# An S4 backward pass woven into an FFN: small gradient stores as rows, parameter work moved out of the middle phase, turns and sums a step apart

## Chip, cores and metric

One core of a Trainium2 chip. The metric is the device time of one execution in microseconds (us), median of several runs. TensorE, VectorE, ScalarE, GpSimd and SyncE appear in the profile as PE (matmuls) and PEld (weight loads), DVE, ACT, POOL and SP. All runs quoted here are in the same (fast) state; the granted TensorE clock of each is named where it matters.

## The reference

The function is a sum of two branches over a layer norm of `u` (2048 x 576): an S4 convolution and a gated FFN of width 4608. The kernel returns the output and twelve gradients (cut):

```python
def _A_ref(u, A_re, A_im, B_re, B_im, C_re, C_im, log_dt, Dskip):   # the six: (576, 128); the last two: (576,)
    dt = jnp.exp(log_dt)[:, None]
    logdA = dt * (A_re + 1j * A_im)
    dB = dt * (B_re + 1j * B_im)
    P = jnp.exp(logdA[:, :, None] * l[None, None, :])               # l = 0..2047
    K = jnp.einsum("dn,dnl,dn->dl", C_re + 1j * C_im, P, dB).real
    ...                                                              # y = irfft(rfft(u) * rfft(K)), padded to 4096
    return y + u * Dskip[None, None, :]
...
return x + _A_ref(xn, ...) + _B_ref(xn, W_gate, W_up, W_down)        # xn = layernorm(x)
# wanted: the value and jax.vjp of it with grad_out
```

## The kernel before

The FFN's matmuls are the backbone. The S4 branch is a Python generator whose steps are emitted between them: each `yield` gives the step's estimated us, and a pace loop asks for the next step while S4's sum lags behind `PACE` times the FFN's. Phase 1 takes FFTs of the inputs, phase 2 builds the kernel K and the sums for the parameters' gradients, in five chunks of 128 channels, phase 3 does the rest of the convolution. Both branches share every engine's in-order queue. In the cuts, dk is the gradient with respect to K; a turn is the transposing of Y into YT, and the sums are the matmuls at L760 that read YT and dkc.

```python
while s4_open and stt < PACE * (ft - start):          # PACE = 0.93
    r = next(sgen, None)
    ...
        stt += r

# the end of phase 1
for n2 in range(ST):                                  # 16 steps
    o = up.tile([P, D], BF16, name="dk_o")
    for hs, ps in self.back2(bp, "dk", n2):           # loads bC from C_dk (2 buffers), multiplies
        g.bal.copy(o[:, hs], ps, DH)
    nc.sync.dma_start(self.dk_dram[:, n2, :], o[:])
    yield 0.5

# phase 2
for k, d0, dsz in dchunks():                          # 5 chunks
    raw = rawp.tile([P, 6, N], BF16, name="raw")
    for i, nm in enumerate(names):
        nc.sync.dma_start(raw[:dsz, i, :], self.aps[nm][d0:d0 + dsz, :])
    ...                                               # ldt, dt = exp, VectorE products -> pw
    Tt = par2.tile([P, 4, P], F32, name="Tt")
    ps = self.ps()
    for i in range(4):
        nc.tensor.transpose(out=ps[:, i * P:i * P + dsz], in_=pw[:dsz, i, :], ...)   # L666
    ...
    for s0 in range(0, dsz, SC):                      # 32 channels
        dkc = parp.tile([P, 2, ST, SC], BF16, name="dkc")
        nc.sync.dma_start(dkc[:, 0, :, :], self.dk_dram[:, :, dd0:dd0 + SC])
        nc.gpsimd.tensor_tensor(dkc[:, 1, :, :], dkc[:, 0, :, :], lv..., op=ALU.mult)
        ...                                           # ex, X, XC; for each 4 channels E, Y
                if len(pend) > 1:
                    self.group(pend.pop(0), ytp, gp)
                    yield 1.5
    ...
    yield from self.param_grads(d0, dsz, raw, dt, Tt, Sm, parp, par2, gp)

def group(self, item, ytp, gp):
    ...                                               # matmuls for K, copy to Kst
    ...                                               # 8 transposes of Y into PSUM
    YT = ytp.tile([P, 2, DG, P], BF16, name="YT")
    bal.copy(YT[:]..., tb, 2 * DG * P, fp32=False)
    ...
    nc.tensor.matmul(gv[:, dl, :, ri, :], lhsT=YT[:, ri, dl, :], rhs=dkc[:, :, :, dd + dl], ...)  # L760
    ...                                               # VectorE: pr = X * sums; Sm = reduce(pr)

# the end of param_grads
dldb = pool.tile([P, 1], BF16, name="dldb")
v.tensor_scalar(dldb[:dsz], tot[:dsz], dtk, None, op0=ALU.mult)
nc.sync.dma_start(self.outs["log_dt"][d0:d0 + dsz].rearrange("(p o) -> p o", o=1), dldb[:dsz])
```

The skip gradient is stored the same way, once near the start, by five stores of one bf16 element per partition from GpSimd's queue.

## Time and profile before

| | before |
|---|---|
| time, median of 6 runs | 2232.35 us (2230.11 to 2234.6) |
| profiled span, mean clock | 2232.9 us, 0.946 |
| TensorE / VectorE / ScalarE busy | 86 / 66 / 68% |

TensorE is the busiest engine, so the reader looks for where it idles. The prediction below shows the page, TensorE's waits, the windows at the dips and the slow transfers.

### The profile page before, as it was taken

Reading aid. Unit: us, or ns where it says so; the run is one execution under the profiler, and the core shown is the slowest. Engines: PE = TensorE matmul, PEld = TensorE weight load, DVE = VectorE, ACT = ScalarE, POOL = GpSimd, SP = SyncE. Lnnn points to the kernel's source line nnn. Section 1 sums busy time; section 2 is a strip of 40 time slices with the busy share of each in tenths; the row PEclk is TensorE's granted clock in tenths of the full one; section 3 lists DMA queues with packets and bytes.
Section 4 is the critical chain, followed back from the end, with each engine's and each line's share of the span. In section 5 each row is a group of like instructions: output and inputs, shape, how many; then the busy total and the mean of one; then the engine's idle time right before and its main releaser. Section 6 shows DMA issues by size and latency. Waiting matters only on the chain. (4 is left out here: it accounts for less than half of the span.)

```text
span 2232.9 us, 45610 instructions
## 1 busy us (share of the span) xinstructions
PE 1929.9 (86%) x17720; PEld 1316.7 (59%) x17720; DVE 1471.0 (66%) x3464; ACT 1518.7 (68%) x3293; POOL 233.0 (10%) x300
## 2 busy tenths in 40 slices
PE   6989999848996999878999699996988998789877
PEld 3665667435754666645666476664665566457545
DVE  7434664499866988569786698747943775652464
ACT  4755766479966979759978699946955764353462
POOL 5210000001100101101101000200100010010010
PEclk9989999969997999989999899998999999899999
DMA  9587889604645644734645554635468996896697
GB/s 281 179 215 243 242 239 274 172 8 94 145 100 78 127 114 95 149 75 74 130 113 97 90 117 106 132 99 78 88 142 262 259 257 209 273 317 140 159 248 203
DMA packets 244169, 358.67 MB, mean 161 GB/s; under 512 B 88880, under 2 KB 153520, under 8 KB 243184
## 3 DMA queue, kind: packets, MB, share of 16 engines
q1 hardware_dynamic: 213136, 292.04, 43.8%
q0 software_dynamic: 28704, 61.36, 18.9%
q8 instruction: 138, 2.26, 0.4%
q10 hardware_dynamic: 2112, 2.36, 0.3%
q14 instruction: 79, 0.65, 0.1%
HBM read 211.21 MB, written 144.48 MB: 159 GB/s over the span
## 5 line engine op out<-in xcount | busy, mean ns | idle before, releaser
L65 ACT CAST osx<-ps_mm 128x288 bf16<-128x288 f32 x711 | 270.6, 430 | 88.3 <-PE ps_mm L278 78.7
L283 POOL DMA_DIRECT2D acc_dram<-osx x176 | 152.2, 865 | 1387.8 <-ACT osx L65 1098.7
L278 PE MATMUL ps_mm<-wgT,dgT 128*128 128x288 bf16 x1152 | 218.8, 291 | 9.0 <-DVE upm L243 5.4
L278 PE MATMUL ps_mm<-wuT,duT 128*128 128x288 bf16 x1152 | 217.4, 291 | 0.0
L312 PEld LDWEIGHTS <-xs 128*128 128x128 bf16 x1536 | 151.1, 100 | 109.5 <-issue 15.8
L278 PE MATMUL ps_mm<-wd,hT 128*128 128x288 bf16 x1152 | 190.8, 291 | 22.8 <-ACT upb L241 16.3
L234 PE MATMUL ps_mm<-xT,wg 128*128 128x512 bf16 x720 | 204.2, 389 | 6.7 <-ACT osx L65 3.9
L234 PE MATMUL ps_mm<-xT,wu 128*128 128x512 bf16 x720 | 200.4, 387 | 1.4 <-ACT osx L65 1.1
L234 PE MATMUL ps_mm<-gT,wdT 128*128 128x512 bf16 x720 | 194.3, 387 | 8.1 <-DVE upm L243 8.1
L298 PE MATMUL ps_mm<-gq,hN 128*128 128x144 bf16 x2304 | 169.1, 231 | 22.0 <-DMA gq<-gq_dram 15.0
L764 DVE TENSOR_TENSOR pr<-X,ps_s 128x256 f32<-128x256 f32 x288 | 108.7, 418 | 107.2 <-PE ps_s L760 105.4
L298 PEld LDWEIGHTS <-hN 128*128 128x128 bf16 x2304 | 157.3, 100 | 31.2 <-issue 16.4
L243 DVE SCALAR_TENSOR_TENSOR upm<-ps_mm,upb 128x512 bf16<-128x512 f32 x144 | 99.0, 687 | 91.0 <-ACT upb L241 90.7
L312 PE MATMUL ps_mm<-dgN,xs 128*128 128x384 bf16 x768 | 151.7, 339 | 5.7 <-DMA xs<-xs_dram 5.7
L65 ACT COPY YT<-ps_s 128x1024 bf16<-128x1024 bf16 x140 | 146.4, 1046 | 9.0 <-PE ps_s L753 7.8
L65 ACT CAST obw<-ps_mm 128x384 bf16<-128x384 f32 x101 | 48.2, 478 | 149.8 <-PE ps_mm L312 112.2
L278 PEld LDWEIGHTS <-hT 128*128 128x128 bf16 x1152 | 110.6, 99 | 60.9 <-issue 23.7
L312 PE MATMUL ps_mm<-duN,xs 128*128 128x384 bf16 x768 | 141.5, 330 | 0.0
L278 PEld LDWEIGHTS <-dgT 128*128 128x128 bf16 x1152 | 113.1, 100 | 40.9 <-issue 11.8
L278 PEld LDWEIGHTS <-duT 128*128 128x128 bf16 x1152 | 113.5, 100 | 29.3
L760 PE MATMUL ps_s<-dkc,YT 128*128 128x32 bf16 x1152 | 88.7, 232 | 45.3 <-POOL dkc L677 19.7
L760 PEld LDWEIGHTS <-YT 128*128 128x128 bf16 x1152 | 66.2, 111 | 90.0 <-ACT YT L65 65.2
(245 smaller groups left out, 4262.0 us busy)
## 6 DMA issues: line engine op xcount, KB each, us to landing
acc_dram<-osx POOLq DMA_DIRECT2D x192, 288.0 KB, 5.6
gT<-gT_dram SPq DMA_DIRECT2D x44, 640.0 KB, 6.2
xT<-xT_dram SPq DMA_DIRECT2D x44, 640.0 KB, 5.4
gq<-gq_dram SPq DMA_DIRECT2D x48, 576.0 KB, 4.2
xs<-xs_dram SPq DMA_DIRECT2D x48, 512.0 KB, 3.8
out_dram<-obw SPq DMA_DIRECT2D x96, 96.0 KB, 2.7
base_dram<-base SPq DMA_DIRECT2D x16, 576.0 KB, 4.6
f_base<-base_dram SPq DMA_DIRECT2D x16, 576.0 KB, 5.8
```

The costliest lines, as they stand in the source:

```text
L65: self.nc.scalar.copy(out, in_)
L234: nc.tensor.matmul(ps[:], lhsT=w[:, k, fs], rhs=rhs[:, k, :], start=(k == 0), stop=(k == NK - 1))
L243: nc.vector.scalar_tensor_tensor(upm[:], ps_g[:], 0.0, upb[:], op0=ALU.is_gt, op1=ALU.mult)
L278: nc.tensor.matmul(ps[:, :DH], lhsT=lt[:, js], rhs=rh, start=(i == 0), stop=(i == len(mms) - 1))
L283: nc.gpsimd.dma_start(g.acc_dram[:, t, :, :], o[:], accum_op=ALU.add)
L298: nc.tensor.matmul(ps[:, (ft - f) * 144:(ft - f + 1) * 144], lhsT=self.hN[:, st, ft * P:(ft + 1) * P], rhs=gq[:, st, :], start=(st == 0), ...
L312: nc.tensor.matmul(ps[:, :Fc], lhsT=xs[:, st, :], rhs=src[:, st, :], start=(st == 0), stop=(st == ST - 1))
L760: nc.tensor.matmul(gv[:, dl, :, ri, :], lhsT=YT[:, ri, dl, :], rhs=dkc[:, :, :, dd + dl], start=True, stop=True)
L764: nc.vector.tensor_tensor(pr[:], X[:, dx:dx + DG, r0:r0 + 2].rearrange("p d r a -> p d (r a)").unsqueeze(2).to_broadcast(sh), psg[:, 0:DG ...
```

## The change

The intent: store the small gradients as rows through a transpose; take the raw parameters out of phase 2, with the transposed values and the summed gradients going through memory (`T_dram`, `R_dram`); put one step between turning Y and the sums that read it; let the GpSimd copy dk into the operand instead of the load writing it. The core of the diff:

```diff
-PACE = 0.93
+PACE = 0.95
+def store_rows(g, pool, cols, out):
+    ps = g.psum_s4.tile([P, 512], F32, name="ps_s4")
+    nc.tensor.transpose(out=ps[:NK, 0:P], in_=cols, identity=g.ident_f[:])
+    rowb = pool.tile([NK, P], BF16, name="rowb")
+    nc.vector.tensor_copy(rowb[:], ps[:NK, 0:P])
+    nc.sync.dma_start(out[0:full * P].rearrange("(k p) -> k p", p=P), rowb[0:full, :])
+    nc.sync.dma_start(out[full * P:D].rearrange("(k p) -> k p", k=1), rowb[full:NK, 0:D - full * P])
 def dskip_out(g, small):
-    for k, d0, dsz in dchunks():
-        nc.gpsimd.dma_start(g.out_dskip[d0:d0 + dsz].rearrange("(p o) -> p o", o=1), totb[:dsz, k:k + 1])
+    store_rows(g, small, tot[:], g.out_dskip)
 ... (phase 1)
+        yield from self.params()        # raw loads, products, transposes; Tt stored to T_dram
 ... (phase 2, per chunk)
-                raw, ldt, dt, pw, transposes, copy to Tt
+                nc.sync.dma_start(Tt[:, :, 0:dsz], self.T_dram[:, :, d0:d0 + dsz])
+                    dkr = parp.tile([P, ST, SC], BF16, name="dkr")
+                    nc.sync.dma_start(dkr[:], self.dk_dram[:, :, dd0:dd0 + SC])
-                    nc.sync.dma_start(dkc[:, 0, :, :], self.dk_dram[:, :, dd0:dd0 + SC])
+                    nc.gpsimd.tensor_copy(dkc[:, 0, :, :], dkr[:])
+                            if len(turned) > 0:
+                                self.sums(turned.pop(0), gp)
+                                yield 0.8
                             if len(pend) > 1:
-                                self.group(pend.pop(0), ytp, gp)
-                                yield 1.5
+                                turned.append(self.turn(pend.pop(0), ytp))
+                                yield 0.7
-                yield from self.param_grads(d0, dsz, raw, dt, Tt, Sm, parp, par2, gp)
+                nc.sync.dma_start(self.R_dram[:, :, d0:d0 + dsz], R[:, :, :dsz])
 ... (end of param_grads)
-        nc.sync.dma_start(self.outs["log_dt"][d0:d0 + dsz].rearrange("(p o) -> p o", o=1), dldb[:dsz])
+        v.tensor_scalar(g.dld[:dsz, k:k + 1], tot[:dsz], dtk, None, op0=ALU.mult)
+        if k == NK - 1:
+            store_rows(g, pool, g.dld[:], self.outs["log_dt"])
 ... (phase 3)
+                for k, d0, dsz in dchunks():
+                    raw, dt = self.load_raw(rawp, k, d0, dsz)
+                    yield from self.param_grads(d0, dsz, raw, dt, pool, pool)
```

Also `ytp` grows from 2 to 3 buffers.

More of the change, by code (lines that the diff above doesn't have):

```diff
@@ L87, in make_consts @@
     g.dsk_acc = consts.tile([P, NK, NSG], F32, name="dsk_acc")
+    g.dld = consts.tile([P, NK], F32, name="dld")
+    nc.vector.memset(g.dld[:], 0.0)
 def iota(nc, ap, pattern, base, mult):
@@ L148, in ln_group @@
     return xT, gT
+def store_rows(g, pool, cols, out):
+    nc = g.nc
+    ps = g.psum_s4.tile([P, 512], F32, name="ps_s4")
+    nc.tensor.transpose(out=ps[:NK, 0:P], in_=cols, identity=g.ident_f[:])
+    rowb = pool.tile([NK, P], BF16, name="rowb")
+    nc.vector.tensor_copy(rowb[:], ps[:NK, 0:P])
+    full = NK - 1
+    nc.sync.dma_start(out[0:full * P].rearrange("(k p) -> k p", p=P), rowb[0:full, :])
+    nc.sync.dma_start(out[full * P:D].rearrange("(k p) -> k p", k=1), rowb[full:NK, 0:D - full * P])
 def dskip_out(g, small):
@@ L154, in dskip_out @@
     nc.vector.tensor_reduce(out=tot[:], in_=g.dsk_acc[:], op=ALU.add, axis=AX.X)
-    totb = small.tile([P, NK], BF16, name="dsk_totb")
-    nc.vector.tensor_copy(totb[:], tot[:])
-    for k, d0, dsz in dchunks():
-        nc.gpsimd.dma_start(g.out_dskip[d0:d0 + dsz].rearrange("(p o) -> p o", o=1), totb[:dsz, k:k + 1])
+    store_rows(g, small, tot[:], g.out_dskip)
 class Ffn:
@@ L451, in __init__ @@
         self.dk_dram = d("dk_dram", [P, ST, D])
+        self.T_dram = d("T_dram", [P, 4, D], F32)
+        self.R_dram = d("R_dram", [P, 4, D], F32)
         self.k_dram = d("k_dram", [P, D // 32, ST, 32])
@@ L502, in make_dft128, with load_raw @@
                 nc.sync.dma_start(dram[:], dst[:])
+    def load_raw(self, pool, k, d0, dsz):
+        nc = self.g.nc
+        raw = pool.tile([P, 6, N], BF16, name="raw")
+        for i, nm in enumerate(("A_re", "A_im", "B_re", "B_im", "C_re", "C_im")):
+            nc.sync.dma_start(raw[:dsz, i, :], self.aps[nm][d0:d0 + dsz, :])
+        ldt = pool.tile([P, 1], BF16, name="ldt")
+        nc.sync.dma_start(ldt[:dsz], self.aps["log_dt"][d0:d0 + dsz].rearrange("(p o) -> p o", o=1))
+        dt = pool.tile([P, 2], F32, name="dt")
+        nc.scalar.activation(dt[:dsz, 0:1], ldt[:dsz], ACT.Exp)
+        return raw, dt
@@ new lines, in params, with turn @@
+    def params(self):
+        g, nc, bal = self.g, self.g.nc, self.g.bal
+        v = nc.vector
+        with ExitStack() as c:
+            rawp = self.pool(c, "par_raw", 2)
+            parp = self.pool(c, "par_w", 2)
+            todo = []
+            def turn():
+                pw, d0, dsz = todo.pop(0)
+                Tt = parp.tile([P, 4, P], F32, name="Tt")
+                ps = self.ps()
+                for i in range(4):
+                    nc.tensor.transpose(out=ps[:, i * P:i * P + dsz], in_=pw[:dsz, i, :], identity=g.ident_f[:dsz, :dsz])
+                bal.copy(Tt[:, :, 0:dsz], ps[:].rearrange("p (i d) -> p i d", d=P)[:, :, 0:dsz], 4 * dsz)
+                nc.sync.dma_start(self.T_dram[:, :, d0:d0 + dsz], Tt[:, :, 0:dsz])
+            for k, d0, dsz in dchunks():
+                raw, dt = self.load_raw(rawp, k, d0, dsz)
+                Ar, Ai, Br, Bi, Cr, Ci = (raw[:dsz, i, :] for i in range(6))
+                v.tensor_scalar(dt[:dsz, 1:2], dt[:dsz, 0:1], 1.0 / TWO_PI, None, op0=ALU.mult)
+                pw = parp.tile([P, 4, N], F32, name="pw")
+                p1 = parp.tile([P, N], F32, name="p1")
+                p2 = parp.tile([P, N], F32, name="p2")
+                v.tensor_scalar(pw[:dsz, 0, :], Ar, dt[:dsz, 0:1], None, op0=ALU.mult)
+                v.tensor_scalar(pw[:dsz, 1, :], Ai, dt[:dsz, 1:2], None, op0=ALU.mult)
+                v.tensor_tensor(p1[:dsz], Cr, Br, op=ALU.mult)
+                v.tensor_tensor(p2[:dsz], Ci, Bi, op=ALU.mult)
+                v.tensor_tensor(p1[:dsz], p1[:dsz], p2[:dsz], op=ALU.subtract)
+                v.tensor_scalar(pw[:dsz, 2, :], p1[:dsz], dt[:dsz, 0:1], None, op0=ALU.mult)
+                v.tensor_tensor(p1[:dsz], Cr, Bi, op=ALU.mult)
+                v.tensor_tensor(p2[:dsz], Ci, Br, op=ALU.mult)
+                v.tensor_tensor(p1[:dsz], p1[:dsz], p2[:dsz], op=ALU.add)
+                v.tensor_scalar(pw[:dsz, 3, :], p1[:dsz], dt[:dsz, 0:1], None, op0=ALU.mult)
+                bal.add(d=1.8, a=0.2)
+                todo.append((pw, d0, dsz))
+                yield 2.0
+                if len(todo) > 1:
+                    turn()
+            turn()
+            yield 1.0
@@ L628, in phase2 @@
             iota(nc, lv[:], [[1, ST]], 0, 16)
-            rawp = self.pool(c, "k_raw", 1)
             parp = self.pool(c, "k_par", 1)
@@ L635, in phase2 @@
             yop = self.pool(c, "k_yo", 3)
-            ytp = self.pool(c, "k_yt", 2)
+            ytp = self.pool(c, "k_yt", 3)
             gp = self.pool(c, "k_g", 2)
-            names = ("A_re", "A_im", "B_re", "B_im", "C_re", "C_im")
-            pend = []
+            pend, turned = [], []
             for k, d0, dsz in dchunks():
-                raw = rawp.tile([P, 6, N], BF16, name="raw")
-                for i, nm in enumerate(names):
-                    nc.sync.dma_start(raw[:dsz, i, :], self.aps[nm][d0:d0 + dsz, :])
-                Ar, Ai, Br, Bi, Cr, Ci = (raw[:dsz, i, :] for i in range(6))
-                ldt = rawp.tile([P, 1], BF16, name="ldt")
-                nc.sync.dma_start(ldt[:dsz], self.aps["log_dt"][d0:d0 + dsz].rearrange("(p o) -> p o", o=1))
-                dt = rawp.tile([P, 2], F32, name="dt")
-                nc.scalar.activation(dt[:dsz, 0:1], ldt[:dsz], ACT.Exp)
-                v.tensor_scalar(dt[:dsz, 1:2], dt[:dsz, 0:1], 1.0 / TWO_PI, None, op0=ALU.mult)
-                pw = parp.tile([P, 4, N], F32, name="pw")
-                p1 = parp.tile([P, N], F32, name="p1")
-                p2 = parp.tile([P, N], F32, name="p2")
-                v.tensor_scalar(pw[:dsz, 0, :], Ar, dt[:dsz, 0:1], None, op0=ALU.mult)
-                v.tensor_scalar(pw[:dsz, 1, :], Ai, dt[:dsz, 1:2], None, op0=ALU.mult)
-                v.tensor_tensor(p1[:dsz], Cr, Br, op=ALU.mult)
-                v.tensor_tensor(p2[:dsz], Ci, Bi, op=ALU.mult)
-                v.tensor_tensor(p1[:dsz], p1[:dsz], p2[:dsz], op=ALU.subtract)
-                v.tensor_scalar(pw[:dsz, 2, :], p1[:dsz], dt[:dsz, 0:1], None, op0=ALU.mult)
-                v.tensor_tensor(p1[:dsz], Cr, Bi, op=ALU.mult)
-                v.tensor_tensor(p2[:dsz], Ci, Br, op=ALU.mult)
-                v.tensor_tensor(p1[:dsz], p1[:dsz], p2[:dsz], op=ALU.add)
-                v.tensor_scalar(pw[:dsz, 3, :], p1[:dsz], dt[:dsz, 0:1], None, op0=ALU.mult)
-                Tt = par2.tile([P, 4, P], F32, name="Tt")
-                ps = self.ps()
-                for i in range(4):
-                    nc.tensor.transpose(out=ps[:, i * P:i * P + dsz], in_=pw[:dsz, i, :], identity=g.ident_f[:dsz, :dsz])
-                bal.copy(Tt[:, :, 0:dsz], ps[:].rearrange("p (i d) -> p i d", d=P)[:, :, 0:dsz], 4 * dsz)
-                bal.add(d=1.8, a=0.2)
@@ L674, in phase2 @@
                     dd0 = d0 + s0
+                    dkr = parp.tile([P, ST, SC], BF16, name="dkr")
+                    nc.sync.dma_start(dkr[:], self.dk_dram[:, :, dd0:dd0 + SC])
                     dkc = parp.tile([P, 2, ST, SC], BF16, name="dkc")
-                    nc.sync.dma_start(dkc[:, 0, :, :], self.dk_dram[:, :, dd0:dd0 + SC])
-                    nc.gpsimd.tensor_tensor(dkc[:, 1, :, :], dkc[:, 0, :, :], lv[:].unsqueeze(2).to_broadcast([P, ST, SC]), op=ALU.mult)
+                    nc.gpsimd.tensor_copy(dkc[:, 0, :, :], dkr[:])
+                    nc.gpsimd.tensor_tensor(dkc[:, 1, :, :], dkr[:], lv[:].unsqueeze(2).to_broadcast([P, ST, SC]), op=ALU.mult)
                     ex = xp.tile([P, SC, 40], F32, name="ex")
@@ L728, in phase2, with turn @@
                             yield 2.9
+                            if len(turned) > 0:
+                                self.sums(turned.pop(0), gp)
+                                yield 0.8
                             if len(pend) > 1:
-                                self.group(pend.pop(0), ytp, gp)
-                                yield 1.5
-                while pend:
-                    self.group(pend.pop(0), ytp, gp)
-                yield 1.5
-                yield from self.param_grads(d0, dsz, raw, dt, Tt, Sm, parp, par2, gp)
-    def group(self, item, ytp, gp):
+                                turned.append(self.turn(pend.pop(0), ytp))
+                                yield 0.7
+                while pend or turned:
+                    if turned:
+                        self.sums(turned.pop(0), gp)
+                        yield 0.8
+                    if pend:
+                        turned.append(self.turn(pend.pop(0), ytp))
+                        yield 0.7
+                R = xp.tile([P, SX, 32], F32, name="w1")[:].rearrange("p a b -> p (a b)").rearrange("p (i d) -> p i d", d=P)
+                q1 = xp.tile([P, SX, 16], F32, name="xa")[:].rearrange("p a b -> p (a b)")
+                q2 = xp.tile([P, SX, 16], F32, name="xr")[:].rearrange("p a b -> p (a b)")
+                S_r, S_i, T_r, T_i = Sm[:, 0, :dsz, 0], Sm[:, 1, :dsz, 0], Sm[:, 0, :dsz, 1], Sm[:, 1, :dsz, 1]
+                cr, ci = Tt[:, 2, :dsz], Tt[:, 3, :dsz]
+                a, b = q1[:, :dsz], q2[:, :dsz]
+                v.tensor_copy(R[:, 0, :dsz], S_r)
+                v.tensor_scalar(R[:, 1, :dsz], S_i, -1.0, None, op0=ALU.mult)
+                v.tensor_tensor(a, cr, T_r, op=ALU.mult)
+                v.tensor_tensor(b, ci, T_i, op=ALU.mult)
+                v.tensor_tensor(R[:, 2, :dsz], a, b, op=ALU.subtract)
+                v.tensor_tensor(a, cr, T_i, op=ALU.mult)
+                v.tensor_tensor(b, ci, T_r, op=ALU.mult)
+                v.scalar_tensor_tensor(R[:, 3, :dsz], a, -1.0, b, op0=ALU.mult, op1=ALU.subtract)
+                nc.sync.dma_start(self.R_dram[:, :, d0:d0 + dsz], R[:, :, :dsz])
+                bal.add(d=1.6)
+                yield 1.6
+    def turn(self, item, ytp):
         g, nc, bal = self.g, self.g.nc, self.g.bal
@@ L755, in group, with sums @@
         bal.copy(YT[:].rearrange("p r d n -> p (r d n)"), tb, 2 * DG * P, fp32=False)
+        return YT, X, dkc, Sm, s0, dd, dx
+    def sums(self, item, gp):
+        g, nc, bal = self.g, self.g.nc, self.g.bal
+        YT, X, dkc, Sm, s0, dd, dx = item
         psg = self.ps()
@@ L766, in group, with param_grads @@
         bal.add(d=1.3)
-    def param_grads(self, d0, dsz, raw, dt, Tt, Sm, pool, par2, gp):
+    def param_grads(self, d0, dsz, raw, dt, pool, gp):
         g, nc, bal = self.g, self.g.nc, self.g.bal
         v = nc.vector
-        R = pool.tile([P, 4, P], F32, name="pw")
-        q1 = pool.tile([P, N], F32, name="p1")
-        q2 = pool.tile([P, N], F32, name="p2")
-        S_r, S_i, T_r, T_i = Sm[:, 0, :dsz, 0], Sm[:, 1, :dsz, 0], Sm[:, 0, :dsz, 1], Sm[:, 1, :dsz, 1]
-        cr, ci = Tt[:, 2, :dsz], Tt[:, 3, :dsz]
-        a, b = q1[:, :dsz], q2[:, :dsz]
-        v.tensor_copy(R[:, 0, :dsz], S_r)
-        v.tensor_scalar(R[:, 1, :dsz], S_i, -1.0, None, op0=ALU.mult)
-        v.tensor_tensor(a, cr, T_r, op=ALU.mult)
-        v.tensor_tensor(b, ci, T_i, op=ALU.mult)
-        v.tensor_tensor(R[:, 2, :dsz], a, b, op=ALU.subtract)
-        v.tensor_tensor(a, cr, T_i, op=ALU.mult)
-        v.tensor_tensor(b, ci, T_r, op=ALU.mult)
-        v.scalar_tensor_tensor(R[:, 3, :dsz], a, -1.0, b, op0=ALU.mult, op1=ALU.subtract)
-        Gd = par2.tile([P, 4, N], F32, name="Tt")
+        R = pool.tile([P, 4, P], F32, name="R")
+        nc.sync.dma_start(R[:, :, :dsz], self.R_dram[:, :, d0:d0 + dsz])
+        yield 0.5
+        Gd = pool.tile([P, 4, N], F32, name="Gd")
         ps = self.ps()
@@ L789, in param_grads @@
         nc.scalar.copy(Gd[:dsz].rearrange("p i n -> p (i n)"), ps[:dsz, :])
-        bal.add(d=1.6, a=0.5)
+        bal.add(a=0.5)
         yield 2.0
@@ L794, in param_grads @@
         dtk = dt[:dsz, 0:1]
+        q1 = pool.tile([P, N], F32, name="q1")
+        q2 = pool.tile([P, N], F32, name="q2")
         u1, u2 = q1[:dsz], q2[:dsz]
@@ L820, in param_grads @@
         v.tensor_reduce(out=tot[:dsz], in_=acc[:dsz], op=ALU.add, axis=AX.X)
-        dldb = pool.tile([P, 1], BF16, name="dldb")
-        v.tensor_scalar(dldb[:dsz], tot[:dsz], dtk, None, op0=ALU.mult)
-        nc.sync.dma_start(self.outs["log_dt"][d0:d0 + dsz].rearrange("(p o) -> p o", o=1), dldb[:dsz])
+        k = d0 // P
+        v.tensor_scalar(g.dld[:dsz, k:k + 1], tot[:dsz], dtk, None, op0=ALU.mult)
+        if k == NK - 1:
+            store_rows(g, pool, g.dld[:], self.outs["log_dt"])
         bal.add(d=4.5, a=1.5)
@@ L842, in phase3 @@
                 yield from self.fwd1("k", lambda n2: (lambda n, hf: kk[:, hf * half:(hf + 1) * half, n, :]), None, ap)
+            with ExitStack() as c1:
+                rawp = self.pool(c1, "p3_raw", 2)
+                pool = self.pool(c1, "p3_g", 2)
+                for k, d0, dsz in dchunks():
+                    raw, dt = self.load_raw(rawp, k, d0, dsz)
+                    yield from self.param_grads(d0, dsz, raw, dt, pool, pool)
             sp = self.pool(c, "p3_s", 1)
```

## The prediction

> **What bounds the kernel now.** I read the page first (busy shares, then the 40 slices), then the list of waits of TensorE, then a table of narrow windows at the dips that the slices show, then the DMA issues, and last the waits of VectorE and of the DMA queue on SyncE.
>
> From the page:
>
> ```profile
> PE 1929.9 (86%) x17720; PEld 1316.7 (59%) x17720; DVE 1471.0 (66%) x3464; ACT 1518.7 (68%) x3293; POOL 233.0 (10%) x300
> ...
> PE   6989999848996999878999699996988998789877
> ...
> PEclk9989999969997999989999899998999999899999
> ```
>
> TensorE is the busiest engine: it idles 303 us of 2232.9. The FFN is nearly all matmul, and the S4 branch (phase 1: FFTs of the inputs; phase 2: from about 420 to 1660 us; phase 3: from there to about 2000 us) is woven into it by the pace counter. So time is gained only where TensorE idles or runs at a low clock. The slices have dips at about 450, 670, 950, 1230, 1510 us. Who ends TensorE's idle time:
>
> ```profile
> PE ps_s L666 <- DVE pw L653: 24.7, 4, 15.0
> PE ps_s L666 <- DVE pw L658: 21.7, 2, 15.6
> PE ps_s L760 <- POOL dkc L677: 19.7, 11, 3.1
> PE ps_s L760 <- ACT YT L65: 18.0, 40, 2.5
> ...
> PE ps_s L666 <- DVE pw L654: 15.2, 1, 15.2
> ```
>
> The three L666 rows are one thing: the float32 transposes of the S4 parameters, which open each chunk of 128 channels, waited 24.7 + 21.7 + 15.2 = 61.6 us, in pieces of up to 15 us. Windows around these places, and three others (after the D-skip output, after the last chunk, at the start of phase 2):
>
> ```profile
> core 0: us, PE busy (x) PEld busy (x) DVE busy (x) ACT busy (x) POOL busy (x), PEclk, DMA share, GB/s
> 125.00:135.00 10.00, 4.01 (x23) 2.81 (x23) 3.60 (x8) 2.17 (x5) 0.56 (x1) 0.61 0.89 173
> 665.00:685.00 20.00, 4.36 (x30) 2.87 (x28) 2.14 (x11) 3.07 (x7) 1.11 (x2) 0.62 0.75 41
> 943.00:963.00 20.00, 4.10 (x28) 2.41 (x26) 1.32 (x5) 4.66 (x8) 0.00 (x0) 0.67 0.43 31
> 1225.00:1245.00 20.00, 6.73 (x37) 4.03 (x36) 3.45 (x14) 4.68 (x11) 0.85 (x1) 0.70 0.85 41
> 1500.00:1525.00 25.00, 7.33 (x33) 3.02 (x31) 4.83 (x20) 3.41 (x6) 0.00 (x0) 0.69 0.69 56
> 1670.00:1685.00 15.00, 7.63 (x28) 3.64 (x29) 0.79 (x3) 0.46 (x2) 0.00 (x0) 0.66 0.74 293
> 448.00:490.00 42.00, 16.11 (x195) 11.83 (x193) 38.72 (x88) 28.23 (x50) 1.27 (x1) 0.54 0.05 7
> ```
>
> In the four chunk boundaries (rows 2 to 5) no engine works: TensorE, VectorE and ScalarE all stand still, the DMA engines are busy at 0.43 to 0.85 of their time, yet move only 31 to 56 GB/s. That is a DMA stall, and it moves tiny pieces. The last row is another kind: VectorE is busy 38.7 of 42 us and TensorE starves. The DMA issues name the culprit:
>
> ```profile
> raw<-in_A_A_im_dram SPq DMA_DIRECT2D x4, 32.0 KB, 17.4
> ...
> ldt<-in_A_log_dt_dram SPq DMA_DIRECT2D x4, 0.2 KB, 3.2
> out_dram<-dldb SPq DMA_DIRECT2D x4, 0.2 KB, 17.7
> ```
>
> The gradient of log_dt, 128 single bf16 elements, one per partition, takes 17.7 us to land. Beside it the next chunk's raw parameters are loaded, and land as late (17.4 us; in the first chunk, with no such store ahead, 1.7 us at the least). VectorE needs raw, TensorE's transposes need VectorE, and the FFN's matmuls stand in the same in-order queue behind them. Reading the same layout is cheap (3.2 us for ldt): only the scattered write is slow.
>
> **What the Trainium skill says.** "DMA: Bandwidth & Descriptors", rules for kernel authors: a non-contiguous last dimension becomes one descriptor per element; its specifications say that writes under 512 B become read-modify-write. The trace agrees for the write (0.2 KB in 17.7 us) and not for the read (3.2 us). The same page, "Issuing engines are not separate DMA queues": all queues share 16 DMA engines; so the D-skip store issued by GpSimd can also hold up others, and DMA share is indeed 1.37 at 37 GB/s between 115 and 120 us. "TensorE: Matmul & The Clock Gate", what's actually happening: after an idle window of about 3.4 us the array falls to half clock and needs about as long a busy one to recover. The trace agrees: the granted clock reads 0.50 from 670 to 685 us, then 0.81. "SBUF — State Buffer", who interferes with whom: a VectorE operation with two SBUF inputs contends with GpSimd. The trace agrees: the product at L659, 0.29 us elsewhere, took 1.02 us at 424.3 us while GpSimd's dkc product ran.
>
> **The change, part by part.** Loss is counted against 93% busy, which TensorE has in phase 2 away from the dips (704.7 of 755 us over four windows).
>
> 1. log_dt's gradient is collected and stored once, as rows (one transpose, two contiguous stores), and raw parameters leave phase 2. Four boundaries span 85 us: 79 us would be busy, 4.36 + 4.10 + 6.73 + 7.33 = 22.5 are. That is 56.5 us, plus the half clock on those 22.5 us (granted about 0.67), 7.4 us: 64 us. I take all of it, because no scattered write and no raw load is left there.
> 2. After the last chunk (1670 to 1685): 14 - 7.6 = 6.3, and 2.6 for the clock, 9 us. The big reload of the kernels (1152 KB, 10.3 us to land) remains, so I take 5.
> 3. D-skip as rows: 125 to 135 loses 9.3 - 4.0 = 5.3, and 1.6 for the clock. I take 4, as its link to the store is only in time.
> 4. Parameters to phase 1, gradients to phase 3. Per chunk some 11 VectorE operations of 0.29 us and about 24 of 0.3 us move away from phase 2: about 50 us of VectorE in all. In phase 1 VectorE is busy 131 of 270 us and in phase 3 191 of 310, so there it is free. It shortens the S4 chain at the boundaries, and with it the bursts after them, where S4 catches up with VectorE at its limit. The burst at 448 to 490 loses 39 - 16.1 = 23, and 7 for the clock: 30 us. Its chain (first raw load at 416.3 to the first exponent product at 427.0, 10.7 us) becomes a load of Tt of some 4 us. I take a third, 10 us, and 5 at the later boundaries.
> 5. turn and sums apart, by one step. The sums at L760 waited 19.7 + 18.0 + 4.8 (a VectorE copy of YT) = 42.5 us. 13.8 of these lie in 430 to 520, where VectorE is the limit and nothing is won. In the calm windows they are 4.9 of 140 us and 6.9 of 225 us, so some 25 us in all. The 1.05 us copies of YT are then done a group earlier. For dkc, a load of 3.7 us is taken out of the chain, and a GpSimd copy put in, like the product beside it at 1.15 us. I take half: 12 us.
> 6. Costs. 18 GpSimd copies, each able to delay one VectorE operation by 0.73 us: 13 us of VectorE, of which I count 3. Tt from memory at each boundary, some 4 us, mostly under FFN work: 4. R and the second raw load in phase 3, five times: TensorE can wait for R as it does there for bC (13.3 us in 6 waits): 5. The second load is 0.9 MB in 256 B pieces in a phase whose DMA share is 0.86: 2. Sum 14.
> 7. PACE. Adding up the yields of both versions by hand, S4 ends at 1245.6 FFN units before and 1243.4 after: S4's count grows from 1109.9 to 1131.4 and 0.95 cancels it. The tail after 2000 us should not move: 0.
>
> Sum: 64 + 5 + 4 + 15 + 12 - 14 = 86 us. 2232.35 - 86 = 2146.
>
> **Rivals.** (a) The stall goes, but VectorE takes its place: phase 2 has VectorE busy 625 and ScalarE 664 of 755 us in calm windows, and VectorE at 92% in the burst. If each saved microsecond only brings the next burst nearer, half of part 1 and all of 4 and 5 are lost: 32 + 15 + 12 = 59 us, 2205. Against it: in the standstills VectorE does nothing too, so it gains the same time, and 50 us of its work leave. (b) The new round trips through memory put waits at the same places: Tt and R, 10 loads, each exposed for its 4 us on TensorE's in-order queue, some 40 us in place of my 9: about 2177. For it: TensorE waits for bC in phase 3 today. Against it: nothing slow is ahead of them, and Tt has two buffers. (c) Everything couples better than I count: the burst at the start of phase 2 goes fully, and L760's waits too: 20 + 13 us more, 2113. (d) The store wasn't the cause and the small 256 B loads are: then the stall moves into phases 1 and 3: about 2200. The first chunk's loads, which landed fast, speak against it.
>
> **Range and chances.** Parts 1 to 3 are measured losses and sum to 73 us; with nothing else won and the costs in full it is 2173, and with half of (b) on top near 2188. With (c) it is near 2110. So 2146, from 2108 to 2182. 2% is 44.6 us, at 2187.7; only (a) or (d) nearly whole gets there: faster 0.92, same 0.07, slower 0.01.
>
> **What would show it.** The L666 waits of some 62 us should be gone, with nothing over 5 us for Tt or R; no DMA should take over 10 us to land but the big ones; clock at the old boundaries 0.95 or more. L760 should wait under 25 us in all. Mean clock should rise from 0.946 to about 0.96, TensorE's idle time fall from 303 to about 225 us. Wrong would be: long waits at new transposes in phase 3, a longer VectorE-bound burst, or the standstill of all engines still there after a boundary.

## More of the kernel before

One line more is wanted later, from the list of VectorE's waits in the kernel before: the instruction that waited, what released it, then us in total, times, longest us.

```profile
DVE pr L764 <- PE ps_s L760: 105.4, 72, 5.2
```

VectorE waited 105.4 us for the sums on TensorE, in 72 pieces. And three 50 us windows of the kernel before: the burst at the start of phase 2 and two calm ones. In each row: start:end, length, then the busy us (with the number of instructions) of PE, PEld, DVE, ACT and POOL, the granted clock, the DMA share and GB/s.

```profile
450.00:500.00 50.00, 23.41 (x264) 17.06 (x265) 46.91 (x110) 36.21 (x66) 1.59 (x2) 0.59 0.04 6
800.00:850.00 50.00, 47.58 (x505) 31.40 (x503) 45.55 (x105) 39.44 (x83) 5.74 (x3) 1.00 0.39 96
1050.00:1100.00 50.00, 45.71 (x432) 31.33 (x431) 42.32 (x98) 45.98 (x101) 7.89 (x9) 1.00 0.62 124
```

In the first row VectorE is the limit (46.91 of 50 us) and TensorE does 23.41 at a clock of 0.59. In the calm rows TensorE has 47.58 and 45.71 of 50.

## The result and the profile after

| | before | after |
|---|---|---|
| median | 2234.48 us (2230.11 to 2240.16, 16 runs) | 2111.05 us (2109.55 to 2117.18, 8 runs) |
| profiled span, clock | 2232.9 us, 0.946 | 2108.8 us, 0.966 |

The ratio is 0.9451 (95% interval 0.9439 to 0.9464). The gain is 2234.48 - 2111.05 = 123 us; 86 were forecast.

The page of the changed kernel, busy times, TensorE's slices and the clock's:

```profile
PE 1901.4 (90%) x17722; PEld 1313.9 (62%) x17722; DVE 1466.5 (70%) x3463; ACT 1525.1 (72%) x3304; POOL 233.8 (11%) x313
...
PE   6989999864899999999999999999888997899877
...
PEclk9999999985999999999999999999999998999998
```

The dips at 670, 950, 1230 and 1510 us are gone. TensorE idles 2108.8 - 1901.4 = 207 us, down from 303. What is left in the middle is one dip, in the ninth and tenth slice, and a slow end. TensorE's waits of the changed kernel for what the change touched:

```profile
PE ps_s L829 <- ACT YT L65: 13.5, 16, 2.3
...
PE ps_s L846 <- DMA R<-R_dram: 1.7, 3, 0.8
```

The sums (now L829) wait 13.5 us for YT and have no row for dkc any more, after 42.5 us. The gradient transposes in phase 3 (L846) wait 1.7 us for R. The parameter transposes (L541, now in phase 1) wait 0.7 us for VectorE in the same list, where they had 61.6 us. VectorE's waits:

```profile
DVE pr L833 <- PE ps_s L829: 40.3, 31, 4.7
...
DVE ex L720 <- DMA Tt<-T_dram: 5.2, 1, 5.2
```

Its wait for the sums fell from 105.4 to 40.3 us. Tt from memory cost one wait of 5.2 us. Two rows of the changed kernel's DMA issues (size of each, us to landing):

```profile
Tt<-T_dram SPq DMA_DIRECT2D x4, 256.0 KB, 5.4
...
raw<-in_A_A_im_dram SPq DMA_DIRECT2D x8, 32.0 KB, 2.4
```

The raw loads that took 17.4 us land in 2.4 us, although they still move 256 B per partition and there are twice as many of them. The same windows of the changed kernel, with one more at the start of phase 2:

```profile
450.00:500.00 50.00, 25.14 (x262) 17.92 (x261) 45.97 (x102) 37.54 (x71) 2.71 (x3) 0.60 0.14 37
500.00:550.00 50.00, 35.05 (x315) 23.05 (x313) 47.80 (x110) 41.30 (x80) 5.97 (x6) 0.74 0.26 50
800.00:850.00 50.00, 48.37 (x464) 33.19 (x465) 41.23 (x94) 49.56 (x108) 7.66 (x9) 1.00 0.48 85
1050.00:1100.00 50.00, 48.93 (x535) 35.21 (x533) 44.81 (x98) 42.68 (x78) 1.62 (x2) 1.00 0.44 111
```

The calm rows sum to 97.3 of 100 us for TensorE, against 93.3 before. The burst at the start has not shrunk: two windows instead of one with VectorE at 46 to 48 of 50 us and a clock of 0.60 and 0.74. Part of the second window is only its later start, but from 350 to 600 us, which holds all of the burst in both kernels, TensorE is busy 199.8 us before and 193.0 us after.

So three questions are left for the chip: is the scattered store alone the cause of the standstills, what is each other part worth, and why did the burst stay.

### The profile page after: what moved, and what is told of

Same layout as the page of the kernel before. It is cut to its first block, busy times and chain, and to the rows that moved or that the text cites. A ratio compares the mean times of both kernels' runs of the same rounds, so it can differ in the third digit from the quotient of the medians.

```text
span 2108.8 us, 45794 instructions
## 1 busy us (share of the span) xinstructions
PE 1901.4 (90%) x17722; PEld 1313.9 (62%) x17722; DVE 1466.5 (70%) x3463; ACT 1525.1 (72%) x3304; POOL 233.8 (11%) x313
## 5 line engine op out<-in xcount | busy, mean ns | idle before, releaser
L65 ACT CAST osx<-ps_mm 128x288 bf16<-128x288 f32 x708 | 278.0, 451 | 56.6 <-PE ps_mm L288 54.1
L308 PE MATMUL ps_mm<-gq,hN 128*128 128x144 bf16 x2304 | 172.7, 232 | 24.6 <-DMA gq<-gq_dram 16.7
L244 PE MATMUL ps_mm<-gT,wdT 128*128 128x512 bf16 x720 | 189.2, 382 | 5.1 <-DVE upm L253 4.2
L244 PE MATMUL ps_mm<-xT,wu 128*128 128x512 bf16 x720 | 193.3, 382 | 0.0
L322 PE MATMUL ps_mm<-dgN,xs 128*128 128x384 bf16 x768 | 146.0, 332 | 4.5 <-DMA xs<-xs_dram 4.5
L833 DVE TENSOR_TENSOR pr<-X,ps_s 128x256 f32<-128x256 f32 x288 | 109.9, 416 | 40.9 <-PE ps_s L829 40.3
L288 PEld LDWEIGHTS <-dgT 128*128 128x128 bf16 x1152 | 112.2, 98 | 41.2 <-issue 13.0
L760 ACT ACTIVATE ysn<-yr 128x512 bf16<-128x512 f32 x144 | 97.0, 674 | 35.1 <-DVE yr L757 34.8
L244 PEld LDWEIGHTS <-wdT 128*128 128x128 bf16 x720 | 69.9, 98 | 79.4 <-issue 8.6
```

What stands on the lines that cost most here:

```text
L65: self.nc.scalar.copy(out, in_)
L244: nc.tensor.matmul(ps[:], lhsT=w[:, k, fs], rhs=rhs[:, k, :], start=(k == 0), stop=(k == NK - 1))
L288: nc.tensor.matmul(ps[:, :DH], lhsT=lt[:, js], rhs=rh, start=(i == 0), stop=(i == len(mms) - 1))
L308: nc.tensor.matmul(ps[:, (ft - f) * 144:(ft - f + 1) * 144], lhsT=self.hN[:, st, ft * P:(ft + 1) * P], rhs=gq[:, st, :], start=(st == 0), ...
L322: nc.tensor.matmul(ps[:, :Fc], lhsT=xs[:, st, :], rhs=src[:, st, :], start=(st == 0), stop=(st == ST - 1))
L760: nc.scalar.activation(sn[:], yr[:], ACT.Sin, scale=-TWO_PI)
```

## The experiments

Each set ran on one chip with its own runs of the kernel before. The median of the kernel before differs between sets (2223.92, 2220.39, 2235.9 and 2217.43 us), while the changed kernel, in the three sets that have it, took 2111.05, 2112.87 and 2112.83. So effects measured against the changed kernel are given in us against 2112.8, and those across sets are marked.

### The log_dt store alone, in the kernel before (e1_rows_only)

```diff
-        dldb = pool.tile([P, 1], BF16, name="dldb")
-        v.tensor_scalar(dldb[:dsz], tot[:dsz], dtk, None, op0=ALU.mult)
-        nc.sync.dma_start(self.outs["log_dt"][d0:d0 + dsz]..., dldb[:dsz])
+        v.tensor_scalar(g.dld[:dsz, k:k + 1], tot[:dsz], dtk, None, op0=ALU.mult)
+        if k == NK - 1:
+            store_rows(g, pool, g.dld[:], self.outs["log_dt"])
```

> The kernel before with one edit: the gradient of log_dt is collected and stored once as rows; the raw parameters are still loaded in phase 2 at every chunk. Theory (the scattered 2-byte store holds up the DMA engines): the raw loads land in under 7 us, the waits of the float32 transposes fall from 61.6 us to under 10, the time falls by 60 to 75 us to about 2165. Rival (the raw loads in 256 B pieces are slow themselves): the waits stay over 45 us and the time within 10 us of before. Second rival (phase 2 is bound by VectorE, so a stall removed is given back in the next burst): the waits go, but the time falls by only about 30 us.

Measured: 2150.52 us (2145.84 to 2153.99) against 2223.92 of before, ratio 0.967 (0.9647 to 0.9694): 73.4 us. The transfer that took 17.4 us, in this run:

```profile
raw<-in_A_A_im_dram SPq DMA_DIRECT2D x4, 32.0 KB, 3.4
```

The raw loads stayed where they were, in phase 2, and land fast. TensorE's waits at the parameter transposes (here L679) fall from 61.6 to 5.3 us in three rows, of which the longest is

```profile
PE ps_s L679 <- DVE pw L666: 3.0, 3, 1.9
```

The store is the cause; the small loads were its victims. Rival (d) falls, and so does the expectation's second rival, that VectorE gives the time back.

### The scattered store put back, in phase 3 of the changed kernel (e2_scatter_late)

```diff
-        v.tensor_scalar(g.dld[:dsz, k:k + 1], tot[:dsz], dtk, None, op0=ALU.mult)
-        if k == NK - 1:
-            store_rows(g, pool, g.dld[:], self.outs["log_dt"])
+        dldb = pool.tile([P, 1], BF16, name="dldb")
+        v.tensor_scalar(dldb[:dsz], tot[:dsz], dtk, None, op0=ALU.mult)
+        nc.sync.dma_start(self.outs["log_dt"][d0:d0 + dsz]..., dldb[:dsz])
```

> The changed kernel with the log_dt gradient stored per chunk as 128 single elements again, now in phase 3. Theory: each such store still takes over 10 us to land and holds up what is issued beside it; five of them within some 60 us, so 25 to 75 us are lost and the time is 2135 to 2185, with new waits of TensorE for R or for the FFN's xs and gq. Rival (the store only hurt because raw loads and their chain of operations were behind it in phase 2): under 10 us are lost.

Measured: 2171.48 us (2167.37 to 2174.78), ratio 0.9771 (0.9747 to 0.9794), some 59 us above the changed kernel (across sets). Its transfers, and a window of 20 us in phase 3:

```profile
out_dram<-dldb SPq DMA_DIRECT2D x4, 0.2 KB, 17.4
raw<-in_A_A_re_dram SPq DMA_DIRECT2D x2, 16.0 KB, 15.8
```

```profile
1560.00:1580.00 20.00, 3.31 (x12) 1.46 (x11) 7.53 (x32) 4.49 (x12) 0.00 (x0) 0.58 0.27 77
```

In the same window the changed kernel's TensorE has 18.94 us. The store takes 17.4 us to land here too, and the loads issued after it come late (15.8 us for the last chunk's; the row counts that chunk's load in phase 1 as well; TensorE waits 16.7 us for an xs of the FFN). The move alone would not have cured this stall: it follows the store.

### The skip gradient scattered again (e6_dskip_scatter)

```diff
-    store_rows(g, small, tot[:], g.out_dskip)
+    totb = small.tile([P, NK], BF16, name="dsk_totb")
+    nc.vector.tensor_copy(totb[:], tot[:])
+    for k, d0, dsz in dchunks():
+        nc.gpsimd.dma_start(g.out_dskip[d0:d0 + dsz].rearrange("(p o) -> p o", o=1), totb[:dsz, k:k + 1])
```

> The changed kernel with the D-skip gradient stored as 5 columns of single elements through GpSimd's queue again. Prediction: 4 us lost. Theory: the store fills the DMA engines for some 10 us near 115 us while little else waits for data, so 2 to 9 us are lost, and the raw loads that now follow it in phase 1 land later, over 8 us. Rival: the standstill at 125 to 135 us came from elsewhere: within 1.5 us of the changed kernel.

Measured: 2122.68 us (2120.82 to 2124.42) against 2112.87 of the changed kernel in the same set: 9.8 us. Two windows of 5 us, and two of the waits from 105 to 140 us:

```profile
115.00:120.00 5.00, 0.00 (x0) 0.00 (x0) 0.00 (x0) 0.00 (x0) 0.00 (x0) 0.92 0.33 30
120.00:125.00 5.00, 0.00 (x0) 0.00 (x0) 0.00 (x0) 0.00 (x0) 0.00 (x0) 0.50 0.17 22
```

```profile
PE ps_mm L291 <- ACT osx L65: 15.6, 1, 15.6
ACT L528 <- DMA ldt<-in_A_log_dt_dram: 15.6, 1, 15.6
```

No engine works for ten us. The loads that follow now are those of the parameters, which the change put right behind this place, and they are on SyncE's queue while the stores are on GpSimd's. ScalarE waits for ldt and VectorE for raw, both in order; the FFN's PSUM evacuation (osx) queues behind on ScalarE, and TensorE waits for it. So the 9.8 us holds for the changed kernel, where these loads follow the store. In the kernel before it was less, as far as windows show: from 100 to 150 us TensorE is busy 41.2 us there and 43.5 us in the changed kernel (e0_after), and its clock of 0.50 to 0.76 from 125 to 140 us is worth some 3 us more, by my estimate from these windows: about 5 us in all.

### Sums straight behind the turn (e3_no_split and e3b_no_split, the same kernel)

```diff
-                            if len(turned) > 0:
-                                self.sums(turned.pop(0), gp)
-                                yield 0.8
                             if len(pend) > 1:
-                                turned.append(self.turn(pend.pop(0), ytp))
-                                yield 0.7
+                                self.sums(self.turn(pend.pop(0), ytp), gp)
+                                yield 1.5
```

> The changed kernel with the sums of a group straight after its turn again, as before. My prediction gave 12 us to this part together with the dk copy: then 2117 to 2123. Theory now: the calm stretches of phase 2 went from 93 to 97 to 98 per cent busy TensorE, some 35 us, and the split is the main reason: 2130 to 2145, with waits of the sums for YT of over 20 us on TensorE and the waits of VectorE's products for the sums near 100 us again.

Measured first: 2113.44 us (2105.24 to 2119.68), ratio 0.9503, which is no loss against 2112.8 in another set, and a miss. It was run again beside the changed kernel (e0b_after, below), in five rounds:

> The changed kernel with the sums placed straight behind their turn again, now on one chip with the changed kernel itself. Theory of the prediction (the split is most of the 12 us of part 5): 8 to 16 us above the changed kernel of this set. Rival (the dk copy is all of part 5; the sums' waits for YT are short and fall while the rest of the list has slack): less than 4 us above. The earlier look, 2113.44 against 2112.87 on another chip, speaks for the rival.

Measured: 2117.43 us (2115.12 to 2120.1), ratio 0.9466 (0.9453 to 0.9479) against 0.9442 (0.9429 to 0.9455): 4.6 us by the medians. It lies between the two expectations. The waits of VectorE for the sums, expected near 100 us again, came to 55.8 us (42.3 in e0b_after), so most of their fall from 105.4 us isn't the split's. The waits of TensorE for YT in this second run:

```profile
PE ps_s L822 <- ACT YT L65: 21.5, 41, 2.4
```

The wait rose from 12.6 us (16 times, in e0b_after) to 21.5 us (41 times): 9 us of waiting, for 4.6 us of time.

### The load straight into the operand (e4_no_dkr)

```diff
-                    dkr = parp.tile([P, ST, SC], BF16, name="dkr")
-                    nc.sync.dma_start(dkr[:], self.dk_dram[:, :, dd0:dd0 + SC])
                     dkc = parp.tile([P, 2, ST, SC], BF16, name="dkc")
-                    nc.gpsimd.tensor_copy(dkc[:, 0, :, :], dkr[:])
+                    nc.sync.dma_start(dkc[:, 0, :, :], self.dk_dram[:, :, dd0:dd0 + SC])
```

(and the product reads `dkc[:, 0]` again)

> The changed kernel without the extra buffer and GpSimd copy for dk: the load goes straight into the operand again and so waits for the sums of the block before. Theory: TensorE waits for GpSimd's dkc product again, about 1.8 us at each of 18 blocks, up to 20 us in all because the split leaves the old operand in use longer: 2120 to 2131. Rival: the load is early enough under FFN work and the time is within 4 us of the changed kernel, the copy being worth nothing.

Measured: 2126.05 us (2118.16 to 2132.05), ratio 0.9559 (0.9528 to 0.9591): about 13 us above the changed kernel (across sets, and the spread is wide), and 12.6 us above e3_no_split of the same set. The wait is back:

```profile
PE ps_s L827 <- POOL dkc L716: 17.3, 8, 4.0
```

So the separate tile is the larger half of part 5: the load may start as soon as the last copy has read dkr, instead of when the last sums have read dkc. The 18 copies of 0.61 us on GpSimd did not eat this.

### Everything but the move (e5_no_move, then e5b_no_move), and its control (e11_yt2)

> All of the change but the move: rows for both gradients, the split, the dk copy, but parameters and parameter gradients stay at the chunk boundaries of phase 2, with the old pace of 0.93. If the parts add up, this is what e1 won (73 us) plus what e3 and e4 lost (12 and 24 us), 109 us, a ratio of 0.951, so the move is worth some 13 us. Theory (the move shortens the chain at each boundary and takes some 50 us of VectorE out of a stretch where VectorE and ScalarE are near their limit): the ratio is 0.951 to 0.958, TensorE dips to 42 to 45 of 50 us at the boundaries and ScalarE and VectorE are at 48 of 50 after them. Rival (the move is worth nothing once the store is fixed): 0.945 to 0.947.

This kernel was refused at the build: without the move there is no room for the third YT buffer. It was mended with 2 YT buffers and with four small tiles laid into existing ones. The edit is the kernel before plus all of the diff but `params()`, `T_dram`, `R_dram` and the gradients in phase 3; in short:

```diff
 # against the changed kernel
-        yield from self.params()
-            ytp = self.pool(c, "k_yt", 3)
+            ytp = self.pool(c, "k_yt", 2)
-                nc.sync.dma_start(Tt[:, :, 0:dsz], self.T_dram[:, :, d0:d0 + dsz])
+                raw, ldt, dt, pw, transposes, copy to Tt      (as before; p1, p2 in the tiles xa, xr)
-                nc.sync.dma_start(self.R_dram[:, :, d0:d0 + dsz], R[:, :, :dsz])
+                yield from self.param_grads(d0, dsz, raw, dt, Tt, Sm, parp, par2, gp, xp)
```

> All of the change but the move: parameters and their gradients stay in phase 2, which begins and ends each group of 128 channels with them; YT has 2 buffers, since the move is what frees room for the third, and four small tiles share room to fit. Theory of the prediction (the move is worth 10 us at the start and 5 us at the later boundaries): 10 to 20 us above the changed kernel of this set, 2121 to 2133 us. Rival 1 (the crowded stretch at the start of phase 2 stayed although the parameters left it, so the move bought little): within 5 us. Rival 2 (the round trips are pure cost): below the changed kernel by 3 us or more. Theory of where the unpredicted 37 us came from, if it is the move: over 30 us above. In the trace, if the move matters, PE idles again near the four later boundaries, over 2 us in each.

The changed kernel itself in this set, and the control with 2 YT buffers alone (`k_yt` 3 to 2):

> The changed kernel again, as the base of this set on its chip. All theories: 2111 to 2117 us as in both earlier sets (2111.05 and 2112.87), 0.945 to 0.952 of the kernel before.

> The changed kernel with 2 YT buffers as before instead of 3, the control for the run without the move. Theory (a turn may run at most one step ahead of its sums, so two buffers suffice): within 3 us of the changed kernel of this set. Rival (the third buffer is what lets the split pay): 5 to 15 us above.

Measured: changed kernel 2112.83 us (2107.59 to 2113.1), control 2110.4 us (2107.26 to 2116.25), without the move 2135.05 us (2132.61 to 2139.48). The third buffer is worth nothing that these runs show. The move is worth 22.2 us, more than the forecast's 15 gross, and well over the 4 that remain of it after its costs (Tt 4, R 5, second load 2). One rival was not run: to fit, this kernel shares tiles (xa, xr) that the kernel before keeps apart, and VectorE's waits for the output copies that read them sum to 20.6 us, against 14.7 in e1_rows_only with tiles of their own. So a part of the 22 us may be the sharing. Where, in windows of the run without the move (first) and of the changed kernel (second), rows: phase 2 without its start, and two pieces at one boundary:

```profile
600.00:1500.00 900.00, 840.19 (x8605) 595.07 (x8672) 750.14 (x1790) 784.06 (x1628) 99.31 (x115) 0.98 0.50 112
1125.00:1150.00 25.00, 23.43 (x214) 15.85 (x218) 13.65 (x41) 20.19 (x46) 5.09 (x6) 1.00 0.49 83
1150.00:1175.00 25.00, 20.41 (x164) 13.07 (x165) 21.02 (x59) 21.82 (x46) 2.56 (x3) 1.00 0.52 99
```

```profile
600.00:1500.00 900.00, 865.27 (x9065) 624.05 (x9137) 761.56 (x1754) 812.38 (x1687) 104.70 (x122) 0.99 0.54 122
1125.00:1150.00 25.00, 23.20 (x204) 15.45 (x204) 23.92 (x57) 23.84 (x57) 5.99 (x7) 1.00 0.71 135
1150.00:1175.00 25.00, 24.16 (x229) 16.85 (x230) 19.20 (x46) 24.68 (x51) 3.41 (x4) 1.00 0.49 95
```

From 350 to 600 us, the start, the move brings TensorE nothing (196.4 us busy without it, 192.0 with it). From 600 to 1500 it brings 865.3 - 840.2 = 25 us, the whole effect. At the boundary VectorE starves first (13.65 of 25 us without the move, 23.92 with it): the chain from sums to gradients is a run of operations of 0.3 us with waits between them, of 2.6 and 2.2 us for ScalarE's output copies and 1.0 us for its copy of the transposes. In the window after it TensorE loses 3.8 of 25 us (20.41 against 24.16), and again at 1200 to 1225 (20.42 against 23.88). I read this as S4 having fallen behind and being issued in a hurry; the windows show the order of the two, not the cause. No single wait shows the loss. Both traces miss about the same number of matmul records (x17577 and x17574, beside 17722 weight loads), so they may be compared.

### The burst at the start (e0_after, e10_both, e9_pace_dk)

My theory after the result: phase 1's last stage is counted 0.5 us per step (8 us in all) and takes from 395.7 to 435.4 us in the changed kernel, 40 us, with TensorE's matmuls of the stage idle 15.8 us for their loads. So S4 enters phase 2 with a debt, and pays it in a burst in which VectorE is the limit. What the trace shows of it: from 469.9 to 512.5 us TensorE runs S4's matmuls alone (L808, L817, L829; eight times the sums), none of the FFN's. The debt isn't in the pace counter, though: adding up the code's yields, S4's sum never lags by more than 5.0 us. So the order on TensorE isn't the one that the counter asks for, and how the work piles up is not shown. Deeper loads and an honest count should remove it:

```diff
-PACE = 0.95
+PACE = 0.97
+            bp2 = self.pool(c, "p1_b2", 4)
-                o = up.tile([P, D], BF16, name="dk_o")
-                for hs, ps in self.back2(bp, "dk", n2):
+                o = bp2.tile([P, D], BF16, name="dk_o")
+                for hs, ps in self.back2(bp2, "dk", n2):
-                yield 0.5
+                yield 2.0
```

> The changed kernel itself, on the chip of the runs beside it, as their yardstick. Every theory: the ratio to the kernel before is that of the first result, 0.945 within 0.003.

> The changed kernel, with the last stage of phase 1 (from the kernel gradient's spectrum back to time) given four buffers in place of two and counted at 2.0 us a step in place of 0.5, with a pace of 0.97 to keep S4's end in place. Theory: the stretch in which VectorE is full and TensorE starves, 445 to 550 us, comes from a backlog: that stage is counted as 8 us and takes some 40, so S4 is behind and then catches up. Then TensorE's loss there falls to under half and the time is 20 to 45 us below the changed kernel. Rival (phase 2 opens with work for VectorE whatever the count): the stretch stays as long and the time is within 8 us.

Measured: the changed kernel 2112.87 us (2110.55 to 2114.59), ratio 0.9516 (0.9499 to 0.9534); with the edit 2090.93 us (2083.75 to 2093.8), ratio 0.9422 (0.9401 to 0.9443). It beats both kernels, by 21.9 us. Two windows of the changed kernel, then with the edit:

```profile
480.00:500.00 20.00, 6.31 (x80) 4.81 (x81) 19.49 (x43) 14.02 (x24) 1.84 (x2) 0.50 0.09 14
500.00:520.00 20.00, 12.38 (x111) 8.88 (x110) 19.11 (x45) 14.28 (x28) 0.88 (x1) 0.53 0.00 0
```

```profile
480.00:500.00 20.00, 19.71 (x185) 13.44 (x184) 19.65 (x46) 18.78 (x43) 3.70 (x5) 0.92 0.28 37
500.00:520.00 20.00, 20.00 (x182) 13.10 (x181) 19.60 (x45) 19.62 (x45) 3.47 (x4) 1.00 0.56 115
```

TensorE gets 39.7 of these 40 us instead of 18.7, with the clock at 0.92 or more. Which half does it? The count alone, with 2 buffers (`yield 2.0` and `PACE` 0.97 of the diff above):

> One half of the run that beat both kernels: the last stage of phase 1 is counted 2.0 per step instead of 0.5 (and PACE 0.97), with 2 buffers as in the changed kernel. The changed kernel took 2111.05, 2112.87 and 2112.83 us in three sets, the run with both halves 2090.93. Theory (the interleaving alone: S4 came late to phase 2 because this stage was counted short): 2088 to 2098 us, and TensorE busy over 14 of 20 us in every window from 440 to 540. Rival (the depth of the loads alone: with 2 buffers the stage's waits for its spectra are what delays S4): 2107 to 2114 us and the crowded stretch with a clock under 0.8 still there. Between, 2098 to 2107: both count.

Measured, in another set: 2103.85 us (2099.24 to 2111.78), ratio 0.9486 (0.9459 to 0.9513), about 9 us below the changed kernel (across sets). The same windows:

```profile
480.00:500.00 20.00, 13.75 (x118) 9.24 (x118) 19.26 (x43) 17.98 (x32) 4.38 (x3) 0.63 0.18 27
500.00:520.00 20.00, 19.99 (x204) 14.10 (x203) 19.96 (x49) 19.95 (x46) 2.53 (x3) 1.00 0.52 114
```

The burst is shorter but still there, with 9.75 us in the window from 460 to 480, so the expected 14 of 20 us in every window was a miss. The stage's matmuls still run from 393.3 to 433.7 us with the count alone; with 4 buffers as well they run from 397.0 to 420.7, and phase 2's first phase product comes at 426.4 instead of 442.7 us (440.6 with the count alone). Both halves count, and the depth of the loads is the larger one as far as sets on different chips can say. The buffers alone were not run, nor the pace of 0.97 alone, which is in both runs.

## Why the prediction was right or wrong

The direction and the range held; the point was 35 us too slow (2146 against 2111.05).

- **Parts 1 and 2, the store (69 us): right.** The store alone gave 73.4 us, and with it TensorE's waits at the parameter transposes fell from 61.6 to 5.3 us. The reading that carried it, all engines still and DMA busy at 31 to 56 GB/s beside a 0.2 KB store of 17.7 us, was the right one ("no engine works" is loose for whole windows: TensorE is busy 4.1 to 7.3 us in each). One clause was wrong: it named the raw loads' departure as part of the gain; they land fast where they were.
- **Part 3 (4 us): near for the kernel before, but half of its worth in the changed one.** Undone there it costs 9.8 us. Only the windows of the kernel before were read, and they show about 5 us; that the change puts new loads behind that store, which a scattered one would have held up, was not thought of.
- **Part 4 (10 us at the start, 5 later): right in kind, wrong in place and size.** The start won nothing; the later boundaries won 25 us of TensorE time. The step that failed is "I take a third, 10 us": it put the burst down to phase 2's own opening chain. The run without the move keeps that chain, and its start is no worse for it (196.4 us of TensorE from 350 to 600 us, against 192.0 with the move), while the edit to phase 1's last stage took 21.9 us off. And the parameters moved into phase 1 delay phase 2: its first phase product comes at 442.7 us, after 428.5 in the kernel before and 414.8 in the run without the move, which has the new pace. At the boundaries "and 5" was a guess without a window behind it.
- **Part 5 (12 us): undersized a little.** The split is 4.6 us and the dk tile about 13, so most of the gain came from dkc, where the expectation for e3_no_split had the split as the main reason.
- **Part 6 (-14 us): oversized.** R cost 1.7 us of TensorE's waits instead of 5, Tt one wait of 5.2 us of VectorE, under which TensorE was busy 5.9 of 6 us (436 to 442). Rival (b) fell with it. The GpSimd copies and the second load were not measured by themselves.
- **Part 7 (0): not tested by itself.** All later kernels kept 0.95 or went to 0.97 with a changed count.
- **What it said would show it** came true in the lists: L760's successor waits 13.5 us (under 25 said), the mean clock is 0.966 (0.96), TensorE idles 207 us (225). One sign missed narrowly: "nothing over 5 us for Tt or R", against VectorE's 5.2 us. "A longer VectorE-bound burst", its sign of a mistake, came true as well, and pointed at part 4.
- **Rival (a)**, VectorE as the new limit, holds for one stretch only, 450 to 550 us, as before the change. Rival (c) named nearly the time that came (2113), but for the wrong reason: it wanted the burst gone, and the burst stayed.

Does it add up? Against the kernel with the rows store alone (2150.5 us), the rest of the change brings 2150.5 - 2112.8 = 37.7 us, where the forecast had 4 + 15 + 12 - 14 = 17. Undone one at a time, skip store, split, dk tile and move cost 9.8 + 4.6 + 13 + 22 = 49 us: more than they bring together, so they overlap; the skip store's 9.8, which needs the move's loads behind it, is one such case. Of the 37 us that the prediction missed, about 21 are this rest, 4 the store, and some 10 the kernel before itself, which took 2234.48 us in the set of the result and 2223.92 in that of the store alone. Why the kernel before drifts by up to 18 us from set to set, on one chip too, while the changed kernel does not, stays open.

## What to carry to other kernels

A store of one element per partition stopped this whole kernel for some 15 us at a time, through the transfers that were issued after it; collect such results and turn them into rows. Where work is woven by a counter of estimated us, check the estimate against the trace stage by stage: here a stage counted 8 us took 40, and counting it 32 us, with a higher pace, took some 9 us off. And the loss from short dependent chains at a boundary appeared here in the windows after it rather than at it, in no single wait, so compare windows, not waits alone, when their worth is to be judged.

## What the Trainium skill lacked or had wrong

- "DMA: Bandwidth & Descriptors", Specifications: it puts transfers under 512 B down as read-modify-write and gives no time for a store of single elements. Here 128 elements of 2 B, one per partition, took 17.4 to 17.7 us to land as a store (18.1 from GpSimd's queue, five in a row) and 64 of them 9.4 to 10.3 us, but 2.9 to 3.2 us as a load of 128; loads in 256 B pieces landed in about 2.4 us in the median. Engines waited 15.4 to 15.6 us for loads issued after such stores (e6_dskip_scatter), although the stores went through another engine's queue.
- "TensorE: Matmul & The Clock Gate", What's actually happening: it gives no share of busy time at which the gate closes. In the burst of the changed kernel the granted clock was 0.50 from 475 to 485 us, although TensorE was busy 4.05 of these 10 us (48 matmuls) and never idle for longer than 1.64 us at a time.
- No page speaks of the drift of a kernel's time between sets on one chip: 2223.92 and 2235.9 us for the kernel before, with spreads of 9.3 and 6.6 us within each.
